# Forming scan states one block later, and holding two deferred weight products behind the first output matmuls

## The chip, the cores and the metric

The kernel runs on one core of one Trainium2 chip. The metric is device time in microseconds (us). Clock figures are the granted TensorE clock as a share of full speed. Engines are called PE (TensorE), DVE (VectorE), ACT (ScalarE), POOL (GpSimd) and SP (SyncE, which in before issues 320 of the 348 transfers).

## The reference, cut to what matters

Two independent computations stand side by side in the output. Part A is a state-space layer with 2048 steps, 1024 inputs and 1024 complex states. Part B is attention with a recurrent memory, in segments of 32 tokens.

```python
# part A
Bu = einsum('bld,pd->blp', x, B_bar)
for t in range(L):  h = Lam_bar * h + Bu[:, t]          # the scan
y = 2.0 * einsum('blp,dp->bld', hseq, Cmat).real + x * Dskip
# part B, for each segment
h = concatenate([mem, xs]);  q, k, v = h @ Wq, h @ Wk, h @ Wv
o = softmax(mask(q k^T * scale)) v @ Wo;  mem = o[:, :M]
return concatenate([a, b], axis=-1)
```

The kernel starts part B from a guess of the memories, made from segment means: a mean of x times Wv ("og") times Wo ("guess"). How it is checked later plays no part here.

## The kernel before

First comes the scan stage: 8 state chunks (`pc`) by 4 time blocks (`tb`). PE alternates the matmuls of part A's scan (L225) with the V projection of part B (L383). DVE does the scan work, and ACT evicts the V projection (`b_vst`) and copies scan results to bf16 (`a_gr`, `a_gi`).

```python
def stage1(self, pc, tb):
    ...                                                  # 16 matmuls (L225), 6 DVE products
    V.tensor_tensor_scan(wr[:], rb, wr[:], ...)          # L237
    V.tensor_tensor_scan(wi[:], rb, wi[:], ...)          # L238
    ...                                                  # carry to the next block
    S.activation(gr[:], wr[:], ACT.Copy); S.activation(gi[:], wi[:], ACT.Copy)   # L248
    ...                                                  # 6 DVE instructions form h
    k.SP.dma_start(self.hs[tb][:, pc, :, :], h[:])       # L258
```

Then comes the output stage. Part A's output matmuls (L289) are added to a skip term by DVE and stored. The V product of the means is done for weight blocks 0 and 1 only here (`og`, L401, "deferred segment means"; blocks 2 to 7 have theirs in the scan stage), and the guess (L414) is worked in between the outputs. The change of stages is called the seam. "State loads" are the loads of part A's states (`a_hl`), "wog loads" those of Wo for the guess (`b_wog`).

```python
def stage2(self, pool):                                  # a generator: two yields per row tile
    ...
    for tt in range(4):
        ot = pool.tile([128, D], BF16, name="a_ot", bufs=2)
        for half in range(2):
            py = k.ps("O")
            ...                                          # 16 matmuls L289
            V.tensor_tensor(ot[:, hs], py[:], xd[:, hs], ALU.add)     # L291
            yield
        k.SP.dma_start(self.out[0, t0:t0 + 128, 0:D], ot[:])          # L293
...
def og(self, hb, w, tag="R"):
    ...                                                  # 32 matmuls of 128x64 (L401)
    k.V.tensor_copy(self.ogT[:, hb * 4:(hb + 1) * 4, :], ...)         # L402, "b_ogT"
def guess(self, pool):
    for q in range(4):
        wo = pool.tile([128, H, 256], BF16, name="b_wog", bufs=2)
        k.SP.dma_start(wo[:], self.Wo[:, :, q * 256:(q + 1) * 256])   # L410, 2 MB
        ...                                              # 2 x 32 matmuls L414 with ogT
...
for i, _ in enumerate(s2):                               # s2 = stage2, g = guess
    if i in (2, 4):  b.og(i // 2 - 1, wv[i // 2 - 1], "P")
    if i > 4 and i % 2 == 1:  next(g, None)
```

A scheduler orders the recorded instructions for each engine. An instruction given to `keep_in_program_order` stays where the program has it.

## Time and profile before

| | before |
|---|---|
| median of 3 runs | 1315.27 us (1313.64 to 1317.27) |
| span of the profiled run, mean clock | 1312.2 us, 0.992 |
| PE busy | 1267.0 us, 97% of the span |
| output stage (start of the last undeferred means at 360.26 us to the end of the last L289 matmul at 494.76 us) | 134.5 us |

PE is the limit, so only its idle or half-clocked time can be won. These are lines of the waits view of PE: who waited for what, us in total, times, longest.

```profile
PE psP L383 <- DMA b_xe<-in_B_x_dram: 11.2, 4, 8.0
PE psP L401 <- DMA b_wv<-in_B_Wv_dram: 10.0, 1, 10.0
PE psP L383 <- ACT b_vst L62: 4.7, 6, 2.9
```

The first wait is mostly the start of the kernel. The second is one wait, which the timeline of PE places between the two stages (start, us, engine, line, operation; in brackets the idle time before it and what ended it):

```profile
360.26 1.10 PE L401 MATMUL psR<-b_xbar,b_wv 128*128 128x64 bf16 x32
361.90 1.09 PE L401 MATMUL psP<-b_xbar,b_wv 128*128 128x64 bf16 x32 [0.54 <-ACT b_vst L62]
372.99 1.89 PE L401 MATMUL psP<-b_xbar,b_wv 128*128 128x64 bf16 x32 [9.99 <-DMA b_wv<-in_B_Wv_dram]
374.69 0.61 PE L289 MATMUL psO<-t_105,a_hl_3617 128*128 128x512 bf16 x1
```

Both deferred means stand ahead of the first output matmul, and the second lacks its weights. The windows view (busy us and number of instructions for each engine, then granted clock, DMA share, GB/s) shows the half clock that follows. It also shows that the DMA engines are busy all through both stretches (share 0.98 and 1.07).

```profile
366.00:378.00 12.00, 4.79 (x40) 2.97 (x42) 0.53 (x2) 0.00 (x0) 0.00 (x0) 0.57 0.98 266
385.00:403.00 18.00, 17.90 (x110) 8.67 (x111) 3.46 (x5) 0.00 (x0) 5.47 (x3) 1.00 1.07 297
```

The waits view of ACT shows what the first part of the change aims at: ACT stands at a copy until DVE's scan is done, and the evictions that PE needs come after the copy in ACT's order.

```profile
ACT a_gr L248 <- DVE a_wr L237: 72.1, 31, 7.2
ACT a_gi L248 <- DVE a_wi L238: 24.9, 31, 1.8
```

### The profile page before, as it was taken

To read this page: it belongs to the slowest core of one execution; us is meant where nothing else is said; L and a number is where in the kernel's file an instruction comes from. 1 tells how busy PE (TensorE), PEld (TensorE's weight loads), DVE (VectorE), ACT (ScalarE), POOL (GpSimd) and SP (SyncE) were. 2 spreads that over 40 slices of the span, in tenths; PEclk is the share of its full clock that TensorE was granted. 3 is DMA by queue.
4 is the path that set the end of the run, shared out by engine and by line. 5 is a ranking of instruction groups with operands and counts; after the bars stand their busy time and mean duration, and the time that the engine had idled before them with its cause. 6 is when DMAs were issued, how large, how long until landed. Compare 5 with 4: busy or idle time off the path is not lost. (4 is left out here: it accounts for less than half of the span.)

```text
span 1312.2 us, 20083 instructions
## 1 busy us (share of the span) xinstructions
PE 1267.0 (97%) x7808; PEld 658.2 (50%) x7874; DVE 673.7 (51%) x1500; ACT 427.1 (33%) x1135; POOL 211.4 (16%) x291
## 2 busy tenths in 40 slices
PE   6899899999969999999999999999999989999997
PEld 2344444444435545555555555555555544444443
DVE  6999998988821224555555555545555530001000
ACT  3333333343210001554544454544544540001000
POOL 5000000000112221222222222222222220000000
PEclk9999999999989999999999999999999989999999
DMA  9993443344389519323343434333333470403000
GB/s 227 262 215 105 121 127 101 110 129 144 121 263 311 172 48 262 85 84 110 99 133 99 133 99 133 99 87 98 86 90 78 142 240 18 136 18 127 16 21 21
DMA packets 230939, 163.15 MB, mean 124 GB/s; under 512 B 74976, under 2 KB 214864, under 8 KB 230840
## 3 DMA queue, kind: packets, MB, share of 16 engines
q1 hardware_dynamic: 229368, 158.18, 42.2%
q0 software_dynamic: 1408, 3.61, 0.9%
q8 instruction: 63, 1.03, 0.3%
q14 instruction: 36, 0.29, 0.1%
q10 hardware_dynamic: 64, 0.02, 0.0%
HBM read 95.72 MB, written 49.30 MB: 111 GB/s over the span
## 5 line engine op out<-in xcount | busy, mean ns | idle before, releaser
L383 PE MATMUL psP<-b_wv,b_xe 128*128 128x512 bf16 x1024 | 229.8, 381 | 16.0 <-DMA b_xe<-in_B_x_dram 11.2
L519 ACT ACTIVATE b_e<-psS 99x396 bf16<-99x396 f32 x176 | 88.2, 501 | 416.8 <-PE psS L516 413.6
L522 POOL TENSOR_TENSOR b_m<-b_e,maskB 99x396 bf16<-99x396 bf16 x160 | 139.4, 871 | 352.9 <-ACT b_e L519 352.9
L542 DVE TENSOR_TENSOR b_ot<-psO,b_r 128x384 bf16<-128x384 f32 x176 | 98.1, 558 | 189.2 <-ACT b_r L536 170.4
L383 PEld LDWEIGHTS <-b_xe 128*128 128x128 bf16 x1024 | 100.0, 98 | 139.3 <-DMA b_xe<-in_B_x_dram 12.7
L607 PEld LDWEIGHTS <-b_ol 128*128 128x128 bf16 x896 | 87.8, 98 | 106.3 <-issue 1.7
L64 DVE CAST b_ost<-psP 128x512 bf16<-128x512 f32 x16 | 11.1, 692 | 193.4 <-PE psP L607 193.4
L62 ACT ACTIVATE b_vst<-psP 128x512 bf16<-128x512 f32 x128 | 73.8, 586 | 97.0 <-PE psP L383 82.8
L607 PE MATMUL psP<-t_4704,b_ol 128*128 128x512 bf16 x438 | 99.6, 381 | 0.7 <-issue 0.2
L607 PE MATMUL psP<-wo_12095,b_ol 128*128 128x512 bf16 x438 | 98.8, 379 | 0.5
L536 ACT ACTIVATE b_r<-b_ln 128x396 f32<-128x396 f32 x176 | 94.0, 534 | 5.4
L535 ACT ACTIVATE b_ln<-psR 128x396 f32<-128x396 f32 x176 | 86.9, 494 | 0.0
L62 ACT ACTIVATE b_ost<-psP 128x512 bf16<-128x512 f32 x16 | 9.6, 597 | 211.2 <-PE psP L607 198.0
L291 DVE TENSOR_TENSOR a_ot<-psO,a_xd 128x512 bf16<-128x512 f32 x32 | 22.1, 692 | 95.6 <-PE psO L289 88.2
L64 DVE CAST b_k_4709<-psP 128x480 bf16<-128x480 f32 (+2 forms) x96 | 48.8, 529 | 31.1 <-PE psP L492 30.6
L540 PE MATMUL psO<-b_m,b_v 99*128 99x99 bf16 x704 | 61.4, 209 | 0.8 <-DMA b_v<-b_vx_74 0.8
L531 PE MATMUL psR<-b_m,ones 99*128 99x396 bf16 x176 | 59.2, 336 | 3.1 <-POOL b_m L522 2.2
L64 DVE CAST b_k_4717<-psP 128x480 bf16<-128x480 f32 (+2 forms) x96 | 48.7, 528 | 21.2 <-PE psP L492 21.2
L540 PEld LDWEIGHTS <-b_v 99*128 99x128 bf16 x704 | 50.6, 98 | 14.3 <-DMA b_v<-b_vx_74 1.1
L64 DVE CAST b_q_4705<-psP 128x480 bf16<-128x480 f32 (+2 forms) x96 | 48.7, 528 | 17.2 <-PE psP L492 17.2
L64 DVE CAST b_q_4713<-psP 128x480 bf16<-128x480 f32 (+2 forms) x96 | 48.6, 528 | 12.5 <-PE psP L492 12.5
L248 ACT ACTIVATE a_gr<-a_wr 128x512 bf16<-128x512 f32 x32 | 20.2, 630 | 72.1 <-DVE a_wr L237 72.1
(724 smaller groups left out, 1950.2 us busy)
## 6 DMA issues: line engine op xcount, KB each, us to landing
b_wv<-in_B_Wv_dram SPq DMA_DIRECT2D x16, 1024.0 KB
b_wog<-in_B_Wo_dram SPq DMA_DIRECT2D x4, 2048.0 KB
out_dram<-a_ot SPq DMA_DIRECT2D x16, 256.0 KB
t_4704<-in_B_Wo_dram SPq DMA_DIRECT2D x1, 4096.0 KB
b_ol<-b_os_90 SPq DMA_DIRECT2D x4, 1024.0 KB
b_ol<-b_os_91 SPq DMA_DIRECT2D x4, 1024.0 KB
b_ol<-b_os_92 SPq DMA_DIRECT2D x4, 1024.0 KB
wo_12095<-in_B_Wo_dram SPq DMA_DIRECT2D x1, 4096.0 KB
```

The lines of the kernel that those rows point to most:

```text
L62: self.S.activation(out, in_, ACT.Copy)
L64: self.V.tensor_copy(out, in_)
L291: V.tensor_tensor(ot[:, hs], py[:], xd[:, hs], ALU.add)
L383: k.PE.matmul(p[:], self.xe[:, c, t * 128:(t + 1) * 128], w[:, c, :], start=(c == 0), stop=(c == KC - 1))
L519: k.S.activation(e[:], s[0:GW], ACT.Exp, scale=float(E) ** -0.5, accum_out=self.accE[0:GW, i:i + 1])
L522: k.G.tensor_tensor(m[:], e[:], mask[0:GW, :, :].unsqueeze(2).to_broadcast([GW, 2, 2, GW]), ALU.mult)
L531: PE.matmul(sm[:, 0:W4], k.ones[0:GW, :], mf, start=True, stop=True)
L535: k.S.activation(ln[:], sm[:, 0:W4], ACT.Ln)
L536: k.S.activation(r[:].rearrange("p a b q -> p (a b q)"), ln[:], ACT.Exp, scale=-1.0, accum_out=self.accR[:, i:i + 1])
L540: PE.matmul(o[:, gg, hh, :], vt[:, 2 * u + gg, hh * 128:(hh + 1) * 128], m[:, gg, hh, :], start=True, stop=True)
L542: V.tensor_tensor(ot[:, :, 2 * u * GX:(2 * u + 2) * GX].rearrange("p h (g n) -> p g h n", n=GX), o[:, :, :, 0:GX], r[:, :, :, 0:GX], ALU.mult)
L607: PE.matmul(p[:], lhs, self.wo[half][:, h, :], start=(h == 0), stop=(h == H - 1))
```

## The change

There are two parts. First, the copies, the forming of the state and its store move into `post()`, called one block later, so that ACT need not stand waiting for the scan of the same block. Second, the first matmul of a deferred mean is kept in program order ("the pin"), so that outputs of part A run ahead of it while its weights are on their way.

```diff
+        self.todo.append((pc, tb, wr, wi, tc2, ts2))
+
+    def post(self):
+        ...
+        pc, tb, wr, wi, tc2, ts2 = self.todo.pop(0)
         gr = self.wp.tile(...); gi = self.wp.tile(...)
         S.activation(gr[:], wr[:], ACT.Copy); S.activation(gi[:], wi[:], ACT.Copy)
 ...
-                k.PE.matmul(p[:, ...], w[:, c, ...], self.xbar[:, c, :], ...)
+                mm = k.PE.matmul(p[:, ...], w[:, c, ...], self.xbar[:, c, :], ...)
+                if tag == "P" and h == 0 and c == 0:
+                    k.tc.keep_in_program_order(mm)
 ...
                     a.stage1(pc, tb)
+                    if pc == 0:
+                        a.post() if tb else None
 ...
                     if pc > 0:
-                        for _ in range(4):
+                        for _ in range(2):
+                            next(v, None)
+                        if not (pc == PC - 1 and tb == NB - 1):
+                            a.post()
+                        for _ in range(2):
                             next(v, None)
 ...                                          # after the loops
+            a.post()
+            a.post()
```

The added lines shift the numbers: after the change the scan is L239, the copies L257, the output matmul L298, its addition L300, its store L302, the means L410, b_ogT L413, the wog load L421 and the guess L425.

More of the change, by code (lines that the diff above doesn't have):

```diff
@@ L126, in __init__ @@
         self.Cre, self.Cim, self.logdt, self.Dskip, self.out = Cre, Cim, logdt, Dskip, out
+        self.todo = []
         self.hs = [k.drp.tile([128, PC, 2, TB], BF16, name=f"a_hs{i}") for i in range(NB)]
@@ L246, in stage1 @@
             self.carry = nx
+        self.todo.append((pc, tb, wr, wi, tc2, ts2))
+    def post(self):
+        if not self.todo:
+            return
+        k = self.k; V, S = k.V, k.S
+        pc, tb, wr, wi, tc2, ts2 = self.todo.pop(0)
         gr = self.wp.tile([128, TB], BF16, name="a_gr"); gi = self.wp.tile([128, TB], BF16, name="a_gi")
@@ L400, in og @@
             for c in range(KC):
-                k.PE.matmul(p[:, h * NSEG:(h + 1) * NSEG], w[:, c, h * 128:(h + 1) * 128], self.xbar[:, c, :], start=(c == 0), stop=(c == KC - 1))
+                mm = k.PE.matmul(p[:, h * NSEG:(h + 1) * NSEG], w[:, c, h * 128:(h + 1) * 128], self.xbar[:, c, :], start=(c == 0), stop=(c == KC - 1))
+                if tag == "P" and h == 0 and c == 0:
+                    k.tc.keep_in_program_order(mm)
         k.V.tensor_copy(self.ogT[:, hb * 4:(hb + 1) * 4, :], p[:, 0:4 * NSEG].rearrange("p (h s) -> p h s", h=4))
```

## The prediction

> **What bounds the kernel now.** TensorE: the page's busy table gives PE 1267 of 1312 us. Only its idle or half-clocked time can be won. The waits view for PE lists 10.0 us for b_wv at the segment-mean matmuls (L401), 4.7 for ACT evictions b_vst in the scan stage, 11.2 for b_xe (8.0 of it the start), small rest.
>
> **The seam, 360 to 378 us (timeline).** The scheduler put both deferred segment means (64 matmuls of 128x64) before the first outputs of part A. The first runs at 361.9; the second needs b_wv, whose load is issued only at 367.1 and lands at 373.0: PE idle 9.99 us. The inputs of part A (a_hl) were issued on the POOL queue by 355 and landed in 4.7 to 6.1 us, so PE could have worked from 361.4. The clock is then half for 10 us (0.53 in 373-378, windows view): a_hl matmuls come every 430 ns against 216. [...]recovering at 377.7 after work resumed at 373.0 (4.7 us).
>
> **What the pin does.** The instruction order shows 48 output matmuls (10.4 us) first, then 32 mean matmuls, 32 outputs, 32 mean matmuls. The second means are reached near 361.4 + 80 x 0.216 + 1.1 = 380, after b_wv lands. Saved: 0.5 + 10.0 wait, plus half of the 4.7 us at half clock (2.35): **12.9 us**, all on the critical path, since PE has no later slack. Given-back check: b_wog landed at about 379 and is now needed near 384; the second quarter of states landed by 386, needed near 393; slack stays at least 5 us although DMA is about 100% busy there (windows view).
>
> **What the state deferral does.** ACT's a_gr/a_gi copies keep their places among the b_vst evictions but take the previous block's scan, so "ACT a_gr <- DVE a_wr" (72.1 us, 31 times) and a_gi (24.9) should nearly vanish. But PE stopped only where ACT held back evictions: 4.7 us, at 108-147 us. There DVE is 100% busy (50.8 of 51 us) and some 8 us behind PE. The largest stop (2.9 us at 143.8) ends when an a_tabc table on ACT waits for DVE's L232 of block 12; summing DVE's instruction times in both orders, I get the same DVE work before that point. So the earlier stops (1.8 us) go, and that last one grows by about as much: **0 us, at most 3**. After 147 us PE is 99.5% busy in the scan stage: nothing to win.
>
> **Predicted:** 1315.3 - 12.9 - 0.4 = **1302 us**, range 1298.8 to 1305.5. Faster by over 2%: 0.02; within 2%: 0.97; slower: 0.01.
>
> **What would show it.** Right: the 10 us PE wait on b_wv gone, no half clock near 370 (mean clock rises from 0.992 to about 0.996), part A's first output matmul near 361.5, not 374.7; later stages unchanged, 13 us earlier. ACT's waits for a_wr fall from 72 to under 10 us. PE's b_vst waits merge into one of about 4 us near 144; PE resumes there near 147 as before. Wrong: PE resumes near 144 or earlier (DVE wasn't the limit); a new PE wait on a_hl, b_wog or a_xd in 362-400.
>
> **What would make it wrong.** b_wog or states landing later than I count; DVE stalling on wr, wi (two deep, held one block longer); or DVE running ahead, up to 3 us more.

(A rule about the clock that no run here shows is cut from the text above. No term of its sum goes with it: 0.5 + 10.0 + 2.35 = 12.9 us, and 1315.3 - 12.9 - 0.4 = 1302. The 2.35 is half of the 4.7 us that the trace of before shows as worked at half clock, from 373.0 to 377.7 us; its clock record has the half clock from 367.5 to 377.7.)

## The result, and the profile after

After the change the median is 1317.95 us (1317.72 to 1319.6, 4 runs), beside 1316.27 us (1313.64 to 1317.57, 4 runs) for the kernel before in the same rounds. The ratio is 1.0018, with a 95% interval of 0.9999 to 1.0037: no difference. The predicted 13 us didn't appear, and the span of the profiled run is 1316.0 us at a clock of 0.990.

The waits view of PE after the change:

```profile
PE psS L425 <- DVE b_ogT L413: 12.8, 1, 12.8
PE psP L392 <- DMA b_xe<-in_B_x_dram: 10.0, 2, 8.2
PE psP L392 <- ACT b_vst L62: 4.9, 4, 2.9
```

The wait for b_wv is gone, as predicted, and a new one of 12.8 us stands in its place. The timeline of PE after shows where:

```profile
361.77 1.10 PE L410 MATMUL psR<-b_xbar,b_wv 128*128 128x64 bf16 x32
362.70 1.03 PE L298 MATMUL psO<-t_105,a_hl_3617 128*128 128x512 bf16 x3
...
380.90 1.10 PE L410 MATMUL psP<-b_xbar,b_wv 128*128 128x64 bf16 x32
...
385.29 0.28 PE L425 MATMUL psS<-b_ogT,b_wog 128*128 128x64 bf16 x4
398.40 1.65 PE L425 MATMUL psS<-b_ogT,b_wog 128*128 128x64 bf16 x28 [12.83 <-DVE b_ogT L413]
```

The first output matmul comes 12 us earlier. The second mean at 380.90 doesn't wait. The guess then starts at 385.29: four matmuls run, so the weights b_wog are there, and the other 28 lack b_ogT of the mean that PE finished near 382. The windows view after shows the half clock moved along with the wait:

```profile
366.00:378.00 12.00, 11.95 (x84) 5.94 (x84) 4.00 (x9) 1.16 (x3) 2.12 (x1) 1.00 0.88 253
385.00:403.00 18.00, 4.95 (x43) 2.95 (x42) 1.62 (x3) 0.00 (x0) 4.23 (x2) 0.62 1.13 329
```

PE ended that mean near 382; why did a 0.41 us copy come only 16 us later? This is the timeline of DVE after:

```profile
377.65 0.69 DVE L300 TENSOR_TENSOR a_ot<-psO,a_xd 128x512 bf16<-128x512 f32 x1 [3.03 <-PE psO L298]
397.32 0.69 DVE L300 TENSOR_TENSOR a_ot<-psO,a_xd 128x512 bf16<-128x512 f32 x1 [18.98 <-DMA out_dram<-a_ot]
397.93 0.41 DVE L413 CAST b_ogT<-psP 128x256 bf16<-128x256 f32 x1
```

DVE had the fifth output addition ahead of that copy in its order. It is the first of the third row tile and needs output buffer 0 again, so it waits until the first store has read it. That store is on SP (timeline of SP after, and below it two lines of before):

```profile
369.75 0.44 SPq L421 DMA_DIRECT2D b_wog<-in_B_Wo_dram  x1
370.24 7.97 SPq L286 DMA_DIRECT2D a_hl_3928<-a_hs_71  x1
...
380.15 0.42 SPq L286 DMA_DIRECT2D a_hl_3934<-a_hs_71  x1
380.62 0.43 SPq L421 DMA_DIRECT2D b_wog<-in_B_Wo_dram  x1
382.08 10.86 SPq L302 DMA_DIRECT2D out_dram<-a_ot  x1
```

```profile
384.00 0.34 SPq L293 DMA_DIRECT2D out_dram<-a_ot  x1
386.64 0.43 SPq L410 DMA_DIRECT2D b_wog<-in_B_Wo_dram  x1
```

The store's data was ready at 370.5 us (second addition, 369.81 + 0.69). It is issued from 382.08 on, and its issue takes 10.86 us where the first store of before took 0.34 us. The same thing happens to the state load behind the first wog load (7.97 us, and 8.01 in before). So in the kernel after, what follows a 2 MB wog load on SP has a long issue both times; what makes it long isn't shown by these traces. In the kernel before, SP had the store ahead of the second wog load. In the kernel after, the scheduler put it behind.

By the landings, the long issue isn't what delays the store's data, though. The semaphore updates in the packed trace tell when a transfer of SP had landed: the second wog load at 396.56 us, the store at 397.20, which is 0.12 us before DVE goes on. In before, the state load ahead of the store landed at 386.59 us and the store at 387.27. In these stretches SP's transfers landed in the order of their issue (after: state load 389.54, wog load 396.56, store 397.20, x load 397.91; before: state load 386.59, store 387.27, x load 389.27, wog load 397.66), so what decides here is the store's place in SP's order. The store landed 0.64 us behind its neighbour after its long issue and 0.68 us behind it after the short one.

The output stage lasted 136.3 us (361.77 to 498.10), beside 134.5 before. The sum closes. Before, it lost 0.54 + 9.99 us of waits and half of the 4.7 us worked at half clock (373.0 to 377.7): 12.9 us. After, it lost 12.83 us of waits and half of the 4.1 us worked at half clock (398.4 to 402.5): 14.9 us. That is 2.0 us worse, and the stage is 1.8 us longer.

The waits of ACT that should have vanished are almost unchanged:

```profile
ACT a_gr L257 <- DVE a_wr L239: 65.2, 27, 7.8
ACT a_gi L257 <- DVE a_wi L240: 27.6, 32, 1.5
```

From the starts and ends of the 32 scans and copies in the trace, each a_gr copy starts a median of 0.03 us after its own scan, before and after the change. The scheduler had moved the deferred copies back. The last write of h starts a median of 4.4 us after the end of the a_wr scan in both; only in the first third of the stage is it later (up to 14.9 us against 7.9).

### The profile page after: what moved, and what is told of

Its sections match the earlier page's. It is cut to its first block, busy times and chain, and to the rows that moved or that the text cites. A ratio compares the mean times of both kernels' runs of the same rounds, so it can differ in the third digit from the quotient of the medians.

```text
span 1316.0 us, 20085 instructions
## 1 busy us (share of the span) xinstructions
PE 1268.6 (96%) x7807; PEld 658.5 (50%) x7874; DVE 673.5 (51%) x1500; ACT 427.3 (32%) x1135; POOL 211.7 (16%) x291
## 5 line engine op out<-in xcount | busy, mean ns | idle before, releaser
L300 DVE TENSOR_TENSOR a_ot<-psO,a_xd 128x512 bf16<-128x512 f32 x32 | 22.1, 691 | 106.3 <-PE psO L298 79.9
L64 DVE CAST b_q_4705<-psP 128x480 bf16<-128x480 f32 (+2 forms) x96 | 48.6, 527 | 17.2 <-PE psP L503 17.2
```

The costliest lines, as they stand in the source:

```text
L64: self.V.tensor_copy(out, in_)
```

## The experiments

Eighteen kernels ran, all with correct results, each with three rounds beside the kernel before. In the first group of expectations T1 is the theory that the order on SP (the wog load ahead of the store) makes the new stall, and T2 the rival that the transfers are simply saturated. Later groups state theirs. "Stage" is the length of the output stage as defined above, from the profiled run. None of the kernels is more than 2% from before, so what is said of gains below is read from the intervals: clear of noise means that the interval doesn't hold 1.

| kernel | median (low to high), us | ratio to before, 95% | stage, us | largest PE wait in it, us |
|---|---|---|---|---|
| before | 1316.27 (1313.64 to 1317.57) | | 134.5 | b_wv 10.0 |
| after | 1317.95 (1317.72 to 1319.6) | 1.0018, 0.9999 to 1.0037 | 136.3 | b_ogT 12.8 |
| pin_only | 1312.2 (1309.8 to 1313.17) | 0.9967, 0.9943 to 0.999 | 129.3 | b_ogT 5.8 |
| defer_only | 1315.33 (1314.95 to 1317.28) | 0.9993, 0.9973 to 1.0014 | 134.6 | b_wv 10.8 |
| out_first | 1310.58 (1309.71 to 1311.99) | 0.996, 0.9938 to 0.9982 | 129.8 | b_ogT 6.0 |
| ot3 | 1309.42 (1305.77 to 1311.08) | 0.9941, 0.9913 to 0.9968 | 128.3 | a_ot 4.5 |
| pin_swap | 1316.5 (1315.08 to 1317.82) | 1.001, 0.9991 to 1.0029 | 135.7 | b_ogT 11.5 |
| defer_held | 1313.87 (1313.07 to 1315.32) | 0.9986, 0.9969 to 1.0002 | 133.4 | b_ogT 9.9 |
| out_act | 1308.75 (1307.55 to 1310.35) | 0.9957, 0.993 to 0.9983 | 128.7 | b_ogT 4.8 |
| out_pool | 1309.85 (1308.97 to 1311.85) | 0.9962, 0.9945 to 0.9979 | 128.8 | b_wog 4.5 |
| ot3_pool | 1310.33 (1309.21 to 1311.79) | 0.9964, 0.9947 to 0.9982 | 128.0 | b_wog 4.0 |
| pin_pool | 1309.59 (1309.23 to 1309.7) | 0.9954, 0.9938 to 0.9971 | 127.7 | b_wog 3.3 |
| pool_wogact | 1309.51 (1308.51 to 1312.67) | 0.996, 0.9937 to 0.9983 | 128.9 | a_ot 5.1 |
| pin_pool_wogact | 1309.65 (1308.56 to 1310.66) | 0.9955, 0.9938 to 0.9973 | 127.6 | a_ot 4.4 |
| first_wqlate | 1312.03 (1308.19 to 1313.35) | 0.9966, 0.9944 to 0.9987 | 130.0 | b_ogT 6.6 |
| pool_wqlate | 1303.52 (1302.71 to 1303.7) | 0.9905, 0.9881 to 0.9929 | 121.4 | none over 2 |
| pin_pool_wqlate | 1303.14 (1302.01 to 1304.09) | 0.9902, 0.9877 to 0.9928 | 121.4 | none over 2 |
| before_tab3 | 1317.34 (1316.38 to 1319.38) | 1.0021, 0.9993 to 1.0049 | 134.7 | b_wv 9.8 |
| after_tab3 | 1318.6 (1318.26 to 1319.96) | 1.0031, 1.0004 to 1.0058 | 136.8 | b_ogT 13.8 |
| best1 | 1311.03 (1310.38 to 1311.93) | 0.9968, 0.9942 to 0.9994 | 129.8 | b_ogT 5.6 |

### Each part of the change alone

pin_only is the kernel before with the pin of `og`. defer_only is the kernel after without it.

```diff
-                if tag == "P" and h == 0 and c == 0:        # defer_only
-                    k.tc.keep_in_program_order(mm)
```

> Theory T1 (order of the transfer queue): the 12.8 us PE wait at the guess matmuls in the changed kernel came from the second b_wog load being issued ahead of part A's first output store; the pin alone keeps the store ahead of b_wog, so that wait is at most 3 us, the half clock near 390-400 is gone, and the time is about 1303 us (1301 to 1307), ratio to before about 0.990. Rival T2 (transfers saturated: part A now asks for its data 13 us earlier than the DMA engines can bring it, whatever the order): a wait of some 10 us between 375 and 400 stays, time 1313 to 1318, ratio about 1.00.

> T1 and my own reading of the scan stage: the state deferral alone changes no wait of PE at the seam (10 us on b_wv as before) and PE resumes near 147 as before, since VectorE is the limit there; if the half-clock window at 146.5 us of the changed kernel belongs to the deferral it shows here too and costs 1.5 us: time 1316 to 1318. Rival: the deferral itself is worth 3 to 5 us in the scan stage and something else hid it: 1311 to 1313.

The deferral alone changes nothing (0.9993, the interval holds 1), and the wait for b_wv stays; its median lies just under the 1316 to 1318 us expected. The pin alone gains a third of a per cent, where T1 expected 1301 to 1307 us. It removes the wait for b_wv and turns up with the same wait for b_ogT, but only 5.8 us of it. SP in pin_only has the store ahead of the second wog load, and the store's issue is short:

```profile
381.00 0.38 SPq L293 DMA_DIRECT2D out_dram<-a_ot  x1
382.38 0.38 SPq L412 DMA_DIRECT2D b_wog<-in_B_Wo_dram  x1
383.71 10.64 SPq L270 DMA_DIRECT2D a_xn<-in_A_x_dram  x1
```

Here it is an x load that stands behind the wog load for 10.64 us, and PE doesn't need that one so soon.

### The order on SP alone

out_first is the kernel after with ordering edges (no semaphore) that put the second wog load, and the first attention weight loads, behind the first store. Orders on PE and DVE are those of the kernel after.

```diff
+                if q == 1:   # and likewise for the first Wq, Wk loads
+                    k.tc.add_manual_dep(wd.ins, k.od.ins.name, <order only>)
```

> The changed kernel with order-only edges that put the second b_wog load (and the first wq, wk loads) behind the first output store on the SP queue; TensorE and VectorE orders are identical to the changed kernel's. T1: the store is issued near 380.6 instead of 382 to 393, the 12.8 us wait shrinks to under 4 us and the half clock at 389-402 goes: about 1304 us (1302 to 1308). T2: the order makes no difference, 1315 to 1319.

The reverse, pin_swap, puts the bad order into the pinned kernel, which has no deferral: first wog load, four state loads, second wog load, store. Two x loads come behind the store as well. PE, DVE, ACT and POOL have exactly pin_only's order.

```diff
+                if tb == 0 and tt == 0:
+                    k.pre(0); hls[1] = load_hl(1); k.pre(1)   # record the loads here
+                    k.tc.add_manual_dep(od.ins, k.w1.ins.name, <order only>)  # store after wog 1
```

> The pin alone (no deferral), with the second wog load placed just ahead of the first output store on SP, as the scheduler placed it in the kernel after; PE, DVE, ACT and POOL order identical to pin_only. T1 (that order is the cause): the issue of the first store is blocked for some 10 us, the b_ogT wait grows from 5.8 us to 11 to 14 us, half clock at the seam from 6.8 to 10 us or more, median 1317 to 1320, 5 to 7 us slower than pin_only. T2 (the deferral itself makes the stall): the wait stays at 5 to 7 us, median within 2 us of pin_only's 1312.2.

out_first gains 0.4% on before (0.996), with the wait for b_ogT down from 12.8 to 6.0 us. pin_swap is as slow as before (1.001), with the wait up from 5.8 to 11.5 us. Its median of 1316.5 us is half a microsecond under the range that was expected, and 4.3 us above pin_only's, where 5 to 7 were expected. Its store stands as in the kernel after:

```profile
377.92 0.43 SPq L422 DMA_DIRECT2D b_wog<-in_B_Wo_dram  x1
378.46 11.92 SPq L303 DMA_DIRECT2D out_dram<-a_ot  x1
```

So the order of two instructions on SP, and not the deferral as such, makes about half of the stall. The other half stays even with the good order, and the expected 1303 us for it was wrong. In out_first the store is issued at 379.77 us, some 10 us after its data is ready (timeline of SP):

```profile
379.77 0.38 SPq L302 DMA_DIRECT2D out_dram<-a_ot  x1
```

It is another 9.5 us until DVE, which needs the buffer, goes on (timeline of DVE of the same kernel):

```profile
389.26 0.69 DVE L300 TENSOR_TENSOR a_ot<-psO,a_xd 128x512 bf16<-128x512 f32 x1 [12.11 <-DMA out_dram<-a_ot]
```

By the semaphore updates, the last state load ahead of the store landed at 388.45 us and the store at 389.14, 0.12 us before that addition. pin_only is alike (390.34 and 391.06). So the half that stays is the same thing again: the store lands behind the state and x loads that SP issued before it.

### A third output buffer

ot3 is the kernel after with `bufs=3` for a_ot.

> The changed kernel with a_ot three deep instead of two; the b_wog load stays ahead of the store and the store is as late as before (issue until about 393). T1: the fifth and sixth a_ot no longer wait for the first store, so b_ogT comes at once after its matmuls and the 12.8 us wait goes or shrinks below 4 us: about 1304 us. If PE really waited for b_wog data (T2) the wait stays: 1315 to 1319.

The wait for b_ogT is gone and 0.6% is gained, so the buffer was what DVE stood for. The median is still 5 us above the 1304 expected: a wait of 4.5 us for a_ot turns up later, at 398.7 us.

### The store on another queue

out_act issues the output stores from ACT in place of SP; out_pool issues them from POOL.

```diff
-                k.SP.dma_start(self.out[0, t0:t0 + 128, 0:D], ot[:])
+                k.nc.scalar.dma_start(self.out[0, t0:t0 + 128, 0:D], ot[:])   # out_pool: k.G.dma_start
```

> The kernel after, with only the part-A output stores (L302) issued from ACT's DMA queue in place of SP's; PE and DVE order at the seam unchanged. Tells apart what holds the first store once it is no longer behind the wog load (out_first still waited 5.95 us for b_ogT and the store was issued only at 379.8 us, after two state loads whose issue blocked SP for 8 us). T1 (head of line: the store is late because SP's queue is blocked by the state and wog loads before it, the transfer itself is short): the store is issued within about 2 us of the first a_ot (near 371 us), lands in a few us, DVE never waits over 3 us for out_dram, the b_ogT wait of PE falls below 1 us, half clock at the seam disappears, median 1303 to 1307. T2 (backlog: the store's bytes queue in the 16 DMA engines behind some 4 MB of state and wog loads whichever queue it goes through): issued early, but lands at about 385 to 390 us; DVE's wait for out_dram and the b_ogT wait of 5 to 6 us stay; median 1309 to 1313, like out_first.

out_act came out between the theories. Its first store was issued at 379.81 us, no earlier than in out_first, although ACT had nothing to do. The line in the timeline of ACT:

```profile
379.81 9.01 ACTq L302 DMA_DIRECT2D out_dram<-a_ot  x3
```

The listing of the built program tells why: the store waits for DVE and also for a DMA semaphore whose last user is the first wog load. Both transfers name the same semaphore, and the wog load landed at 379.73 us, 0.08 us before the store's issue. In the packed traces of before and after, the 324 transfers of SP and ACT name eight semaphores, in turn at 320 of the 323 steps, and POOL's 24 name eight others. The store of the kernel after names that of the first wog load, eight transfers before it, too: the load landed at 382.02 us, and the store was issued from 382.08. From its issue in out_act the store took 6.9 us to land (386.71), DVE went on at 386.83, and PE still waited 4.8 us. So issuing the store from ACT wasn't enough here.

> The kernel after, with the part-A output stores (L302) issued by POOL. In out_act the first store was issued only at 379.8 us although its data was ready at 365.4: its one other wait is for a DMA semaphore that it shares with the wog load issued at 367.3 (eight are handed round over all SP and ACT transfers, and the eighth transfer before it was that wog load, landed about 379.4). POOL's transfers have semaphores of their own. T1 (the store is late only because its issue is held, first by the SP queue, then by the shared semaphore): issued by 367 us, lands within 5 us, the fifth a_ot doesn't wait for out_dram, the b_ogT wait is under 1 us, the 6.8 us of half clock at the seam go, median 1302 to 1306 (12.8 us of stall and some 2 of half clock off 1317.95). T2 (DMA backlog): issued early but landed only at 380 or later, DVE waits 5 us or more for out_dram, median 1308 to 1312 as out_act and out_first.

(The 365.4 us in that text is the first half of the data; in out_act the second half was done at 368.0.) The first store in the timeline of POOL of out_pool:

```profile
369.78 0.60 POOL L302 DMA_DIRECT2D out_dram<-a_ot  x1 [9.69 <-DVE a_ot L300]
```

And the fifth addition in its timeline of DVE:

```profile
380.50 0.69 DVE L300 TENSOR_TENSOR a_ot<-psO,a_xd 128x512 bf16<-128x512 f32 x1 [3.17 <-PE psO L298]
```

The store leaves as soon as its data is there, and the fifth addition waits for PE alone. The stall at the guess is gone (b_ogT no longer among PE's waits), so T1 is right about it: the backlog doesn't hold the store. The store, issued at 369.78 us, landed at 376.70, while the wog load issued on SP at 368.71 landed only at 381.83. T1's marks for the store itself (issued by 367 us, landed within 5 us) were missed by 2 to 3 us, without a wait. But the time expected of T1 is missed too. At 1309.85 us it is T2's, because PE has a new wait, which ends at 420.32 us (waits view of PE of out_pool):

```profile
PE psS L425 <- DMA b_wog<-in_B_Wo_dram: 4.5, 1, 4.5
```

The third wog load is late now, since the guess runs 13 us earlier, and the clock is half for 6.8 us (419.2 to 426.0 us). Two more kernels of that group say the same.

> The same with three a_ot buffers in place of two. T1: nothing left for the third buffer to do, within 1.5 us of out_pool. T2: the third buffer hides the backlog that is left, 3 to 6 us faster than out_pool; the wait of PE for a_ot that ot3 had (4.5 us) shrinks.

> The pin alone (no deferral), with the stores issued by POOL: candidate to beat both kernels. T1: 1302 to 1306, b_wv wait and b_ogT wait both gone, as out_pool within 2 us. T2: 1308 to 1312.

With the store freed, a third buffer adds nothing (0.9964 against 0.9962). The kernel without the deferral gives the same time as the one with it (0.9954 against 0.9962).

### The late third wog load: its queue, or the bytes ahead of it

pool_wogact is out_pool with the wog loads on ACT; pin_pool_wogact is the same on the kernel without the deferral.

```diff
-            k.SP.dma_start(wo[:], self.Wo[:, :, q * 256:(q + 1) * 256])
+            k.nc.scalar.dma_start(wo[:], self.Wo[:, :, q * 256:(q + 1) * 256])
```

> out_pool with the four wog loads issued by ACT in place of SP; order on PE, DVE and POOL the same as out_pool. In out_pool the third wog load was issued at 404.8 us, behind other transfers on SP, although the guess had let its buffer go at about 393 us, and PE waited 4.5 us for it and then ran 6.8 us at half clock. T1 (place on SP's queue): issued by 395 us, landed before it is needed at 416 us, wait and half clock at 419 us go, median 1302 to 1305, which is where the prediction put the change. T2 (bandwidth): the wait stays at 3 us or more or shows up at another load, median 1307 to 1312.

> The pin alone with stores on POOL and wog loads on ACT: the candidate without the deferral. T1: as pool_wogact within 2 us, 1302 to 1305. T2: 1307 to 1312.

T2 in both: the wait for b_wog is gone, and PE waits 5.1 us (4.4) for a_ot instead. DVE there waited for a_xd on POOL, which had waited 17.2 us for an x load. Giving one load a queue only handed the wait to another load here. The test isn't clean: on SP the scheduler also moved the first Wq and Wk loads ahead of the state loads (issued from 370.04 us in pool_wogact, from 393.51 in out_pool), and the third wog load was issued at 400.81 us, later than T1 had it.

pool_wqlate is out_pool with the first four attention weight loads (0.5 MB each, not needed before the attention) behind the third wog load on SP. The other engines have out_pool's order. pin_pool_wqlate is the same without the deferral, and first_wqlate the same on out_first, with the stores on SP.

```diff
+                if hp <= 1:
+                    k.tc.add_manual_dep(ld.ins, k.wd.ins.name, <order only>)   # Wq, Wk after wog
```

> out_pool, with the first four attention weight loads (0.5 MB each) moved behind the third wog load on SP; PE, DVE, ACT and POOL order identical. T1 (the transfers of the stretch 366 to 420 us are saturated, some 300 to 400 GB/s, and 2 MB less is 5 to 7 us less): the third wog load lands before its use at 416 us, its wait (4.5 us) and the half clock at 419 us go, no wait of over 2 us in the output stage, median 1302 to 1305. T2 (the wait comes from the order of dependent steps, not from bytes): a wait of 3 us or more stays, median 1308 to 1311.

> The same on the kernel with the pin alone, without deferral: T1: 1302 to 1305, within 2 us of pool_wqlate. T2: 1308 to 1311.

> out_first (stores on SP, the first ahead of the second wog load), with the four attention weight loads moved behind the third wog load; order on the other engines identical to out_first. The first store is still issued near 380 us, behind the state loads on SP. T1 (the first stall is the late issue of the store, the later ones are bytes): the b_ogT wait of 5 to 6 us stays, median 1308 to 1311, no gain on out_first. T2 (the first stall is bytes too): the wait falls below 3 us, median 1303 to 1306.

pool_wqlate takes 1303.52 us, 0.9905 of before, as T1 had it. The third wog load is issued at 398.05 us and lands at 412.74; in out_pool that was 404.81 and 420.27. The head of its waits view of PE has none of the output stage:

```profile
PE psP L392 <- DMA b_xe<-in_B_x_dram: 10.6, 4, 8.4
PE psP L392 <- ACT b_vst L62: 5.3, 5, 2.9
PE psR L544 <- POOL b_m L535: 2.4, 4, 0.7
```

In its windows view, PE is busy nearly all of the two stretches shown for before and after, at a clock of 1.00:

```profile
366.00:378.00 12.00, 11.95 (x84) 5.95 (x84) 3.90 (x8) 0.72 (x2) 2.74 (x2) 1.00 0.90 261
385.00:403.00 18.00, 17.84 (x165) 9.62 (x165) 3.46 (x5) 0.00 (x0) 8.27 (x7) 1.00 1.08 359
```

Its output stage lasts 121.4 us, 13.1 us less than before; the prediction of 12.9 us was for this. first_wqlate keeps the first stall (6.6 us) and gains nothing on out_first (0.9966 against 0.996; its median is 1 us above the range of T1), so both steps are needed: the store out of SP's queue, and the 2 MB later. Whether those 2 MB hurt as bytes or as entries ahead on SP isn't told apart: in pool_wqlate they leave both. What is shown is that moving the 2 MB helped, and that the wog loads on ACT, with SP's order changed as said, did not. pin_pool_wqlate at 1303.14 us (0.9902) does as well: the deferral adds nothing there either.

### The scan stage: deferral that takes effect, and more table buffers

defer_held is the kernel after with the deferred copies kept in program order, so that the scheduler can't move them back.

```diff
-        S.activation(gr[:], wr[:], ACT.Copy); S.activation(gi[:], wi[:], ACT.Copy)
+        k.tc.keep_in_program_order(S.activation(gr[:], wr[:], ACT.Copy)); k.tc.keep_in_program_order(S.activation(gi[:], wi[:], ACT.Copy))
```

> The kernel after, with the deferred copies gr and gi of each block held in the order in which the program records them. In the kernel after, the scheduler started every gr copy 0.0 us (median) after the scan it reads, as in the kernel before, so the deferral was mostly undone. T1 (the scan stage is limited by DVE's work, 50.8 us busy of 51): the copies now start several us after their scan, ACT's wait for a_wr falls from 65 us to under 15, and yet the stage ends no earlier: part A's first output within 1.5 us of 362.7 us, median within 2 us of after. T2 (the undone deferral is why the stage gained nothing): the stop of 2.9 us near 146.5 us goes and the first output comes 3 us or more earlier.

The copies now start a median of 10.5 us after their scan. ACT's wait for a_wr is gone from its waits view, and that for a_wi is 0.6 us. Between 100 and 160 us PE stops once. This is the line in PE's timeline of before, at the largest of its stops:

```profile
146.68 1.89 PE L383 MATMUL psP<-b_wv,b_xe 128*128 128x512 bf16 x8 [2.88 <-ACT b_vst L62]
```

And the one of defer_held:

```profile
147.08 3.57 PE L392 MATMUL psP<-b_wv,b_xe 128*128 128x512 bf16 x8 [3.14 <-ACT b_vst L62]
```

PE resumes at 147, as before, and the first output comes at 363.29 us, 0.6 us later than after. So T1 is right about the scan stage: the earlier small stops merge into one and nothing is gained. That fits DVE as the limit, busy 50.8 of the 51 us from 96 to 147; no run takes work off DVE there, so this last step is argued and not shown. Its total missed the expected 2 us round the kernel after: it is 4 us faster, 2.9 us of it in the output stage, where the b_ogT wait was 9.9 us and not 12.8. Its SP still has the wog load ahead of the store (issue 10.99 us), but 2 us earlier.

The rival for that stop was the buffers of the trigonometric tables, which ACT may write only once DVE has let them go. before_tab3 and after_tab3 have three sets of them, and best1 is after_tab3 with the stores on ACT.

```diff
-        q = pc % 2
+        q = pc % 3
```

> The kernel before, with three in place of two sets of buffers for the trigonometric tables (pc % 3). Tests the 2.9 us stop of PE near 144 to 147 us. T1 (the table of the next state chunk waits for the last DVE reader of its buffer, two chunks back, and DVE then waits for the table): the stop near 147 us falls below 1 us and the first seam instruction of PE comes 2 to 4 us earlier than 360.3 us; median 1311 to 1314. T2 (DVE is busy 50.8 of 51 us there, so it is the limit by its work alone): the stop stays at 2 to 3 us or moves to another wait on DVE of the same size; median within 1 us of before.

> The kernel after, with three sets of table buffers. T1 (deferral was stopped from helping the scan stage only by the table buffers): the stop near 146.5 us falls below 1 us and part A's first output comes 3 to 5 us earlier than 362.7 us, more than before_tab3 gains. T2 (DVE's work is the limit, and the scheduler moves the deferred copies back to their scans: in the kernel after, a_gr still starts 0.0 us after its scan): no more gain than before_tab3, within 1 us. The seam's b_ogT wait stays at 12 to 13 us in both theories.

> Candidate to beat both: the kernel after with the stores on ACT's queue and three sets of table buffers. T1 of out_act and T1 of the tables both right: 1299 to 1303. Only the store: as out_act. Neither: 1315 to 1318.

The buffers aren't it. The stop comes 9 to 10 us earlier and grows, to 3.98 us (before_tab3) and 4.57 us (after_tab3), and neither kernel is faster. best1 gains only what out_act gained.

## Why the prediction was wrong

- **"Saved: 0.5 + 10.0 wait, plus half of the 4.7 us at half clock: 12.9 us."** Right as a size. The b_wv wait vanished, the first output came at 362.7 us (361.5 predicted), and no half clock stood near 370. With what took the gain away removed, the stage is 13.1 us shorter (pool_wqlate) and the time 1303.5 us, beside 1302 predicted.
- **"All on the critical path, since PE has no later slack", with the "given-back check": this is the step that failed.** It asked only whether data would arrive (b_wog, states), and found 5 us of slack. b_wog was there: four guess matmuls ran at 385.29. What was missing was b_ogT, a 0.41 us copy behind an addition on DVE, which waited for a buffer, which waited for a store that SP had behind a wog load (issue 10.86 us, landed at 397.20, 0.64 us after that load). PE lost 12.83 us there, as much as was to be saved. The listing of the built program shows, before any run, that this load had moved ahead of the store. The check should have followed each operand back through its engine's order and buffers. The list of new waits to look for ("a_hl, b_wog or a_xd") lacks the one that came. Shown by out_first and pin_swap (order on SP), ot3 (buffer) and out_pool (store freed).
- **"Slack stays at least 5 us although DMA is about 100% busy there."** Wrong further on as well. Once the store was freed, the third wog load was 4.5 us late. Work moved 13 us earlier moved the need for data too, and the stretch, with the DMA engines busy all through (share 1.08 from 394 to 422 us in out_pool), didn't deliver earlier.
- **"ACT's waits for a_wr fall from 72 to under 10 us."** Wrong: 65.2. It was taken that code recorded one block later runs one block later; the scheduler moved the copies back. In defer_held, where they do run later, the wait is gone.
- **"State deferral: 0 us, at most 3."** Right, partly for another reason: in the kernel after, the deferral hardly takes effect. Where it does, the predicted picture holds: one stop (3.1 us), PE back at 147.
- **"Later stages unchanged, 13 us earlier."** They are unchanged but no earlier.

The medians of the kernel before moved from 1314.77 to 1316.27 us, with runs from 1312.65 to 1320.58. A single half-clock stretch of 3.4 us near 147 us occurs in some profiles (after, pin_only) and not in others (before, out_first), whatever their kernel. Differences of 1 to 2 us between profiles are not explained here for that reason.

## What to carry to other kernels

When work is moved earlier, everything it needs is needed earlier: follow each operand back through the order of its engine, the buffer it must free and the transfer that frees it, and not only to the arrival of its weights. Before trusting a reordering, compare the instruction order of every engine, the one that issues transfers above all: a small store behind a large load on the same queue landed only after it here (397.20 and 396.56 us), and cost as much as the wait that was removed. Code recorded later isn't executed later unless the scheduler is held to it.

## What else the traces showed of transfers and the clock

- Another queue did more here than save issue time (10.86 us on SP in after, 0.60 on POOL in out_pool). On SP the 256 KB store landed at 397.20 us, right behind the wog load issued before it (396.56), and on POOL's queue it landed at 376.70, 5.1 us ahead of a wog load issued 1.1 us earlier on SP. The stall of 12.8 us behind it went (ratio to before 1.0018, then 0.9962).
- After the change, the stretch in which only 512-byte packets landed (376 to 380 us) moved 290 GB/s in the windows view, that of mostly 4096-byte packets (382 to 384 us) 400. Source and layout differ along with the packet size, so which of them costs the rate isn't told apart.
- Half-clock stretches in the scan and output stages lasted 3.4 us (after, from 146.5 us), 6.8 (out_pool, from 419.2), 10.2 (before, from 367.5) and 13.7 (after, from 388.9). How long PE had waited didn't settle it, by the timeline's modelled matmul ends: the 2.88 us that ended at 146.50 us in after were followed by half clock, the 2.88 us that ended at 146.68 in before were not. After the 3.27 us in pin_pool, 32 matmuls of the guess took 1.89 us, where they took 1.10 before the wait.
